# Gate operations of two groups moved from VectorE to GpSimd, and a new order for every step, in a recurrence followed by an MLP

## The chip, the cores and the metric

The kernel runs on one core of a Trainium2 chip. The core has TensorE (PE, which multiplies matrices; PEld is its loading of weights), VectorE (DVE), ScalarE (ACT) and GpSimd (POOL). SyncE (SP) issues all transfers here. Each engine runs its own queue in order, and engines wait for each other through semaphores. The metric is the time of one execution in device microseconds (us); lower is better.

## The reference

The first part is a recurrence with complex gates, on 4 batches, 8 heads, 768 tokens and a head size of 48. Its output is the input of the second part, an MLP of 3072 tokens, 384 to 2048 to 384, with a leaky rectifier.

```python
mag = np.sqrt(a_re * a_re + a_im * a_im)
scale = np.minimum(mag, 0.999) / (mag + 1e-06)
a_re_n, a_im_n = (a_re * scale, a_im * scale)
for t in range(S):
    new_re = ar * S_re - ai * S_im
    new_im = ar * S_im + ai * S_re
    kv = np.einsum('bhd,bhe->bhde', k[:, :, t], v[:, :, t])
    S_re, S_im = (new_re + kv, new_im)
    y[:, :, t] = np.einsum('bhd,bhde->bhe', q[:, :, t], S_re)
...
h = x @ w_in
g = np.maximum(h, 0.0) + alpha * np.minimum(h, 0.0)
return (g @ w_out).astype(np.float32)
```

The two weight matrices come as 64-bit floats and are made into 32-bit ones in the kernel.

## The kernel before, in words

A gate is split into a magnitude and a phase. The phases are multiplied up along the tokens, and keys and queries are turned by the products; what is left is a recurrence with real decays.

**Gates.** Nine groups of chunks of 128 tokens go through `gates`: in batch 0 one chunk (group 0), two chunks (group 1) and three chunks (group 2), and in each later batch two groups of three. A group loads its gates (L250), normalizes them on ACT and DVE (L253 to L301), multiplies decays into ever longer products (L318) and sends them out (L323, `decs`). Then it multiplies phases up in two levels. Seven pairs of a product (L338) and a sum (L340) run over eight neighbouring tokens; seven pairs of the same lines run over eight such blocks; a loop over the rest carries a running product from one block to the next (again L338 and L340, on `run`), with a copy of the carry from group to group (L381, L387). Then the offsets are multiplied in (L396, L399), scaled to length one (L407 to L411), and put on all tokens with large DVE products (L426, L429), which go out as `phs` (L431). Between these stand short ACT copies (L366, L368, L391, L405, L413). A helper, `small`, sends an operation of at most 80 elements per partition to the engine `tiny`, and a few tiny operations use `tiny_engine` at once; larger ones go to DVE.

**Units.** Each of the 24 chunks is a unit. It loads queries and keys (KQ, L579 and L581), phases (PP, L587, one buffer) and decays (T, L594, two buffers), and turns keys and queries (L661, L663). Then come six levels of block lengths 1 to 32: a DVE product with decays (L717), copies on ACT (L740, L756), products of keys and queries on PE (L678), and masks (L699 on ACT, L702 on DVE). Last come the transposed keys (L785, copied at L787 and L788), the update of the state (L797, L826, L829) and the output (L808 to L841), copied by ACT (L855) and sent to memory (L860, `ysc`).

**MLP.** Finished units are loaded again as `xT` (L873), in groups of one or two. For each group 16 blocks of features are made (L889, three matmuls each), rectified by ACT and DVE (L896, L898), and multiplied with the second weights (L908).

**Weights.** Sixteen pieces are loaded (L491), taken apart on ACT (L507 to L511) and POOL (L515) and put together on DVE (L517, L519).

**Order.** Each of these is a Python generator that yields before every step. A long string of letters, `ORDER`, names whose next step is recorded: A to I are the nine gate groups, J the loads of units, K half rows of the values, L the values, M the pieces of weights, N and O the two weights, P to m (that is P to Z, then a to m) the 24 units, n the loads of `xT`, o the MLP. The order of the string is the order of every engine's queue and of SP's queue. Nothing is reordered at run time: an instruction that waits holds up all behind it on its engine.

Of the kernel before, what the change touches and what calls it, by code (L numbers as in the profile page):

```python
# [27 lines left out]


ORDER = (  # L30
    "AAAAAAAAAAAAAAAAAAAAABAAAAJMJJMABBBMMBANJMMAOAAAAAAAAAAAAAAAAAALLLNBLAAAAAAAAAAALNAAAAAAAKKKKKKKLLLA"
# [4 lines left out]
    "CQRMLLNDCJQCNRNRLLCQCCLLLRMCQCQDQRJJOCOCKQODCCCCRDNQQQQCCQQQQQQJODMQLNNDQODDODoQEKoooooooDOoRooNDJoo"
    "oooooDRRQQRQLLoooDNoooLoRLLLLLDRLOQNQooQoQLooRRoRoDDoQDQDOOLDoooDDoRDELDLRRRRORRRRRJDooDDDDDDDRoooRN"
    "NooDDRooooooEoRDRRRRRDNDoDoESDSDRDJOSREKOoooooLnoLLKoRSoooRRRRSSOLLKLSSSooESRLooooooLRoSOLLoLJELLSoo"
    "NJSSSSoEoEESSDooDDooDDDDDDooooDDDDDDDKJREEoooDDDDooEDDDSDDoEooEoooSSSRSSSoLSooooJJSETSJSJJooKJSoEooo"
    "DDDDDDooDESDSoooSSSDDDSSJEEoEETSSSSDESSSoSSSTEoooooooJJoKoEooDSDTooooEoSoTUKTLoTTTLoooooooooLTLoLoDK"  # L40
    "UooooooLDDTDJJooooJJnKDDDoEEooooDooTTETooDooooooLUoooooooooEoTToooUUDDLoooooooDTooToooooooDLDUUUoooo"
    "ooUTUUooooooUoTTTTEoUUTTTTEooTTUToLLLLoooEEEToLooTTTTTTJJTTUoUUoTTUJoEooTETTTTTKEUUUUUFooooEUoooLLVo"
    "oEoUooLLLELULLUVUoTUTVooUEEoooEULLLLLoooUUUJJJFEEUUUUUJJVVVUVVooooVVVJoUUUUUVVooFVooooUooVVoVFFVVoFV"
    "LLVooEEEEEEEEEEEEEEEEoooEEEEoooooFFJoWVLLVWJFVoooJooooVooVVVVVWVoLVFooWoFoEEEoEVoVLWWLLLLLLELLVWVnVo"
    "oJJEEEEEEJJFWooFEEEEEoWWoFFVFVJVFWVVoFoVooooooEWEWFVLVLVWWVWVVVVoooLKLooLLLoLLLJFFWWoXoWLJoEEoEEELEo"
    "ooooEooJooWWoEWEWWWEoooWEoEoooWWooFoWoWFoooooEXWWoooooLXoFoooooFFXoLXXWWWWXXWXFEXWXWWWXJJoooooJXXJXF"
    "WXXFFFFoWWWWWoXoXooLoooWooooooXWLXXXXXooFoooXXFYoLLFFFFFFFoXXooXoXXoooLLLLLLLoooLLLYXXXJJXFJXFFFFFFF"
    "FFFFooXYGooXXXGooYoooXXnFYJXXYYoFooYYXXXXYGooooYJJJoooooooooooJJYFFFFooJoooJooYYYYLGGoGZYYoooooooGGo"
    "FFFFFFFooooFoYZoooFooFFoZooooZYYZYYZGYYZZoYYYoGZoYFFoYoooKKLLoYLLLLZLoLLLJLFFFFFLFLFFoZGGYoooooGZooG"
    "GoGGYYoYYJJYoKKYGooYFFoFKKYoYLYLYLFLLLLYYLLLLFGaGZoYZFYYYFZZLZGKooooZooooLLoZKooFFFFFoooooZZZZaZZZZZ"  # L50
    "ooooZZoooooZooZoooJJFFGnooJoZZZZZFFFLooLFFZLZoZJLLLoGoaaGooooooooaZZaaGGJoGoooaooaLHaHaooGGoooGGGooa"
    "ooooooooZZaZGGZZZoZaaaaaGGoooaHJoGoooooooaaaoaGGaaGaaaoooooGGaoLoaLoJoooooHHGboGGGGGGGaoHoaooLLobooL"
    "LoooooJHHabJabHaaaaaabaJbJJaJaJaHaaabbbbbbbbHKoooooooHoooooooJGGGGoGGbbbHbGGooocGGGGbJHoooooooooooJG"
    "GGKoooHbbccoooooooooobbccbGGGHcGbobbbGcGoooGGGGGGGGGHccooobbHGbGKLooooHHboobLLJLLLLLoLLLLLbLKnoobbcc"
    "cHbbHJbcbcGHHHbHHbbcJoHHLLLLLLooLoLJLLHHHcooooocccHHoooooooooHGGGGbbbbbbbboGccccccGGocGGooocLoooooGo"
    "cLoccooooocLLGoGHGGooocJoooocGcccccccccccccJcccooKdooHooHoooJJJoHHHoJooHHHodHHHHoooooooooooHHHHdHHHH"
    "HooHHdoodddJdJddddJJooeooooooooooooddoodddoooeoooddHHoooooooooHddeeeeoHHHHHLHHHHHHHLLLdddLLLLLdLLLLo"
    "JLooeeddddodooHHddoJJeoooHdddHdddddneoooHHoIddeeeeeoodeJfLfIHdHHdHeddddooooeHooooLLLLooooooJJoooIIoo"
    "oeooooIoooHoHHHooeeIoeeeHHHLfILoooHIooLooeIofHeJJoeooeooooIfffefoooeeLofoLoLoeLLLeeeeeeeeoJHfKHJJooo"
    "oooofeoILLfooIeeHffffKLLLfoeLooeeeeeooooooofoooooooofoooLoofKffgooooffffffIffLILLLLJooIgHooooLfLfooo"  # L60
    "IooIKKIIIIoffffIfJnJfJHgfgJofIJJooooooofoooooogIfggfgoLoooffIIfLfffIogoKoggooooooooooooohhoogooooggg"
    "ggoIhJhggoooooLoJoooooooooohhLJJooooghggggggghohogIILIIoogIoooggIogLLLLooooooIohhhhhooooLLLLgIoKKggg"
    "ggggggJJJhhooohogggLIoooooooooIIIIIIKKoooogoghoIoooooioooLooooiJJIIoooooonIIIoohhhoiioooIIIIIoIhhhII"
    "hhhLLLLLLLhhhiJiooILLLLLooIhJooohiohhooIIooooiiJhhhhhhIhIIiohooooiooLoLiLLLILiJIhhIhhhhhJiiIiiiiooII"
    "IIIIIIIoooooooooooLiiiiIoIooooohhiiiiiiooojiooIIIIoooooIIoLjJJjjLooooLIooLiLoLLIjjjooooIooijjjjIIooo"
    "ooooiiiIiIIiiooiLooioooLLLiLLILoLLLIIjoiiijjoiiiioooIiojoooooooooojjjoooooooonojjjoooojjLjjjjjoooooI"
    "jLjLLooooooojjoojjjjjjoooJJJJJoooJJoojJJjoooookokkJJoooooooooooojkjkLLjjjkjjojjkkoJkkoJJJkoookooooLL"
    "LooooooooJlJlkkooooooooookokklooklokooooooloolkkkkokkklllLooookookLkoloLJkoooooooooLLkLLkLoLoooollkk"
    "kkkkkkkkkkkkkoooooooooollllllooJoooooookkolooooollollmmnJJloooooooomooollooooooooollmllooooommlloooo"
    "ooooooLLoLLoLoooLLLLLoLLLLooooomooooooommmmmoooollllllooolloooooolllllllllmmoooooooooLooLLLoooommooo"  # L70
# [930 lines left out]
```

## Time and profile before

| | us |
|---|---|
| median of 3 runs | 854.49 (851.1 to 855.48) |
| the profiled execution, in all | 854.34 |
| its span | 852.6 |
| PE busy | 697.3 (82%) |
| DVE busy | 653.5 (77%) |
| ACT busy | 439.1 (52%) |
| POOL busy | 209.2 (25%) |
| DMA packets | 57.1% of 16 queues' span, 129.20 MB |

The profile is of one execution. It tells the busy time of each engine, in the whole and in 40 equal slices of the span (one digit a slice, in tenths), the clock that was granted to PE, groups of instructions with their line, engine, tiles and shape, their number, total time and mean time, the idle time before them and what ended it, and the chain of work that ended last. An idle engine that is not the bottleneck costs nothing.

### The profile page before, as it was taken

To read this page: it belongs to the slowest core of one execution; us is meant where nothing else is said; L and a number is where in the kernel's file an instruction comes from. 1 tells how busy PE (TensorE), PEld (TensorE's weight loads), DVE (VectorE), ACT (ScalarE), POOL (GpSimd) and SP (SyncE) were. 2 spreads that over 40 slices of the span, in tenths; PEclk is the share of its full clock that TensorE was granted. 3 is DMA by queue.
4 is the path that set the end of the run, shared out by engine and by line. 5 is a ranking of instruction groups with operands and counts; after the bars stand their busy time and mean duration, and the time that the engine had idled before them with its cause. 6 is when DMAs were issued, how large, how long until landed. Compare 5 with 4: busy or idle time off the path is not lost.

```text
span 852.6 us, 26860 instructions
## 1 busy us (share of the span) xinstructions
PE 697.3 (82%) x11488; PEld 529.4 (62%) x11488; DVE 653.5 (77%) x1020; ACT 439.1 (52%) x937; POOL 209.2 (25%) x293
## 2 busy tenths in 40 slices
PE   0001314776998899889999999999999999999998
PEld 0001313565776677667777777777777777777776
DVE  5999999997996899599989997887776846633212
ACT  6767758766355754474576436554344334322221
POOL 6131232376403710260056144000052000000000
PEclk9999656798998999999999999999999999999999
DMA  8687876755768365756765766667454555412010
GB/s 238 155 272 188 263 200 189 216 128 138 203 174 199 102 182 163 209 133 156 231 156 145 212 162 177 157 182 185 113 130 104 148 143 117 102 46 65 11 39 9
DMA packets 194174, 130.91 MB, mean 154 GB/s; under 512 B 74120, under 2 KB 185864, under 8 KB 194056
## 3 DMA queue, kind: packets, MB, share of 16 engines
q1 hardware_dynamic: 194056, 129.20, 57.1%
q8 instruction: 90, 1.47, 0.7%
q14 instruction: 28, 0.23, 0.1%
...
## 4 chain that ended last, share of the span: by engine, by line
PE 63%; DVE 18%; POOL 6%; ACT 5%; DMA 4%; issue 3%; SPq 0%; DVEq 0%; ACTq 0%; POOLq 0%
PE ps_o L908 26%; PE ps_h L889 24%; PE ps_lv L678 4%; POOL gate L338 3%; PE ps_y L817 3%; DVE KQ L717 3%; PE ps_kv L797 2%; PE ps_y L841 2%; DVE gate L338 2%; DVE gate L426 2%; DMA T<-decs 2%; POOL run L340 2%; DVE gate L340 1%; PE ps_kt L785 1%; POOL gate L340 1%
## 5 line engine op out<-in xcount | busy, mean ns | idle before, releaser
L908 PE MATMUL ps_o<-w_out_sb,g_sb 128*128 128x384 f32 x768 | 297.9, 500 | 11.7 <-DVE g_sb L898 9.0
L889 PE MATMUL ps_h<-xT,w_in_sb 128*128 128x256 f32 (+1 forms) x1344 | 301.2, 357 | 0.0
L889 PEld LDWEIGHTS ps_h<-xT,w_in_sb 128*128 128x128 f32 x1344 | 235.1, 193 | 72.2 <-issue 3.3
L898 DVE SCALAR_TENSOR_TENSOR g_sb<-g_sb,al,ps_h 128x256 f32<-128x256 f32 (+1 forms) x224 | 97.3, 436 | 133.4 <-ACT g_sb L896 132.7
L896 ACT ACTIVATE g_sb<-ps_h 128x256 f32<-128x256 f32 (+1 forms) x224 | 79.1, 354 | 203.7 <-PE ps_h L889 202.7
L908 PEld LDWEIGHTS ps_o<-w_out_sb,g_sb 128*128 128x128 f32 x768 | 137.9, 192 | 63.0 <-DVE g_sb L898 12.0
L717 DVE TENSOR_TENSOR KQ<-KQ,T 96x1024 f32<-96x1024 f32 x120 | 146.6, 1225 | 33.9 <-PE ps_lv L678 22.9
L678 PE MATMUL ps_lv<-WQ 96*32 96x32 f32 x2304 | 34.3, 202 | 80.4 <-DVE WQ L661 51.8
L678 PEld LDWEIGHTS ps_lv<-WQ 96*32 96x32 f32 x2304 | 26.5, 115 | 98.1 <-DVE WQ L661 51.8
L338 POOL TENSOR_TENSOR gate<-gate 128x72 f32<-128x72 f32 x42 | 26.3, 626 | 148.3 <-ACT gate L368 145.5
L740 ACT COPY WQ<-KQ 96x1024 f32<-96x1024 f32 x48 | 50.0, 1041 | 15.4 <-DVE KQ L717 15.1
L515 POOL TENSOR_SCALAR top<-top 128x768 f32<-128x768 f32 x16 | 39.3, 2461 | 70.0 <-ACT top L507 59.7
L338 DVE TENSOR_TENSOR gate<-gate 128x576 f32<-128x576 f32 (+5 forms) x84 | 50.5, 601 | 1.7
L756 ACT COPY W<-KQ 96x512 f32<-96x512 f32 x48 | 30.8, 642 | 40.6 <-DVE KQ L717 33.1
L855 ACT COPY T<-ps_y 48x256 f32<-48x256 f32 x96 | 30.7, 366 | 36.8 <-PE ps_y L841 36.2
L817 PE MATMUL ps_y<-A,VL 64*48 64x64 f32 x2304 | 42.3, 227 | 3.7 <-issue 3.7
L785 PE MATMUL ps_kt<-ident,KQ 96*128 96x96 f32 x192 | 26.4, 264 | 22.2 <-DVE KQ L717 12.2
L426 DVE TENSOR_TENSOR gate<-gate 128x1152 f32<-128x1152 f32 (+2 forms) x36 | 44.2, 1250 | 0.1
L699 ACT ACTIVATE A<-ps_lv,columns 128x64 f32<-128x64 f32 x144 | 37.4, 337 | 13.0 <-PE ps_lv L678 12.9
L817 PEld LDWEIGHTS ps_y<-A,VL 64*48 64x48 f32 x2304 | 40.6, 128 | 4.4 <-issue 4.4
L785 PEld LDWEIGHTS ps_kt<-ident,KQ 96*128 96x128 f32 x192 | 22.1, 150 | 31.1 <-ACT T L788 10.9
L678 PE MATMUL ps_lv<-KQ,W 96*32 96x32 f32 x1536 | 24.2, 204 | 17.9 <-ACT W L756 17.9
...
## 6 DMA issues: line engine op xcount, KB each, us to landing
...
```

The lines of the kernel that those rows point to most:

```text
L338: on(4 * k).tensor_tensor(out=m, in0=w[:, 1::-1].unsqueeze(2).to_broadcast([P, 2, 2, k]), in1=pairs_of(u), op=ALU.mult)
L426: TT(out=m[:, a], in0=U5[:, 1 + a], in1=turned(off3, o)[:, a].unsqueeze(1).unsqueeze(3).to_broadcast([P, L // 2, nb, 2]), op=ALU.mult)
L515: nc.gpsimd.tensor_scalar(out=top, in0=top, scalar1=F64_SMALL, scalar2=None, op0=ALU.max)
L678: nc.tensor.matmul(t[64 * i + j:64 * i + j + HC // 2, p], lhsT=keys(n, g), rhs=queries(n, g), start=True, stop=True)
L717: nc.vector.tensor_tensor(out=x, in0=x if x0 is None else x0, in1=m, op=ALU.mult)
L740: nc.scalar.copy(z.rearrange("p i n t -> p i (n t)").rearrange("p i (m h) -> p m i h", h=h), bass.AP(tensor=KQ.tensor, offset=KQ.offset + ...
L785: nc.tensor.transpose(t[:, p], KQ[:, 1, 4 * i + p], ident[:D2, :D2])
L817: nc.tensor.matmul(o, lhsT=Vp[h][64 * i:64 * i + 64, s, e_ * D:(e_ + 1) * D], rhs=a, start=False, stop=False)
L889: nc.tensor.matmul(p, lhsT=w_in_sb[:, f // 2, kk, f % 2 * P:(f % 2 + 1) * P], rhs=x_of[m][:, kk], start=(kk == 0), stop=(kk == NK - 1))
L896: nc.scalar.activation(gt, p, AF.Relu, scale=-1.0)
L898: nc.vector.scalar_tensor_tensor(out=gt, in0=gt, scalar=al_1[:, f:f + 1], in1=p, op0=ALU.mult, op1=ALU.add)
L908: nc.tensor.matmul(sums[0], lhsT=gt[:, c * P:(c + 1) * P], rhs=w_out_sb[:, f], start=(f == 0), stop=(f == NF - 1))
```

## The change

The test that picks the engine for tiny operations asks for the first group instead of the first batch. So groups 1 and 2, which are the rest of batch 0, do their operations of at most 80 elements on POOL, as all groups of the later batches already do; group 0 stays on DVE. And the whole of `ORDER` is another string: every queue has a new order. No tile, buffer, shape or transfer is changed.

```diff
 ORDER = (
-    "AAAAAAAAAAAAAAAAAAAAABAAAAJMJJMABBBMMBANJMMAOAAAAAAAAAAAAAAAAAALLLNBLAAAAAAAAAAALNAAAAAAAKKKKKKKLLLA"
-    "OALLAMNNAAAAAAOAAAAAAAAABLBNAAAAAAALAANBBNOOBNBBBLBMBBBJOJNOBBBBBNBBJNNNBBNBBBBOBBBBBBBBBBBBBBBNOPBP"
...
+    "AAAAAAAAAAAAAAAAAAAAAAAAAAMMMAAMMJBBBBAMBJNNNNAAAAAAAAAAAAABABNANAAAAAABAAAABBABBNNAABBMBBABBNAAAABB"
+    "BBBKBAAKKBJNABAKBAKAKAKAKOKNKJKKKKAAAAKOBBBANAABKABOMAABMAAAAABABAAABAAOOOOOOOBNNOOBBNOONNBNMNNNBJJB"
...
-        tiny, tiny_engine = (DVE, nc.vector) if b == 0 else (POOL, nc.gpsimd)
+        tiny, tiny_engine = (DVE, nc.vector) if g < 1 else (POOL, nc.gpsimd)

         def small(k, *after):
             return tiny(k, *after) if k <= SMALL else DVE(k, *after)
```

Here `g` is the number of the group and `b` that of the batch.

More of the change, by code (lines that the diff above doesn't have):

```diff
@@ L30 @@
 ORDER = (
-    "AAAAAAAAAAAAAAAAAAAAABAAAAJMJJMABBBMMBANJMMAOAAAAAAAAAAAAAAAAAALLLNBLAAAAAAAAAAALNAAAAAAAKKKKKKKLLLA"
-    "OALLAMNNAAAAAAOAAAAAAAAABLBNAAAAAAALAANBBNOOBNBBBLBMBBBJOJNOBBBBBNBBJNNNBBNBBBBOBBBBBBBBBBBBBBBNOPBP"
-    "OBPPPPCCCBOKBBBBBBBBBBBBBPPOBBPKBCBBBMPCBPKKBCBJKKOPOPBBBBBBOMBKPNPMBBKNJBCKBBBBPPMBKKNKKBBNBPBBBBPP"
-    "BCCBPPOPCCCPPPNNPPCCCCPPCPPPPJLPPPPPJNCJPCNNNCCNCNCCQJQJPQJDDJJCPCJMNCNCPCPCPPCOCQQPDQDDJPPPPOCOOOCK"
-    "QCQCCCCCCQQCCCCCMOQCOJCJRCCRCOQOCOQQCQCOOOCCCCCCNNKKMMCCOCQCRCQCQCNNNKCLLLLLLQLCCCCCRQOCnCDCCCOCOCCC"
@@ L36 @@
[L36 to L70, printed above, removed]
@@ L71 @@
-    "oooooooooooooLoooooomoooooomooooLLLLLLLLmooonooooooooooommommooooooooooooooooooooooooommmmmmoooooooo"
-    "ooooooooommmooooooooooooooommmmmmmmmmmmomoommnoooooooooooooooooooooooooooooooooooooooooooooooooooooo"
+    "AAAAAAAAAAAAAAAAAAAAAAAAAAMMMAAMMJBBBBAMBJNNNNAAAAAAAAAAAAABABNANAAAAAABAAAABBABBNNAABBMBBABBNAAAABB"
+    "BBBKBAAKKBJNABAKBAKAKAKAKOKNKJKKKKAAAAKOBBBANAABKABOMAABMAAAAABABAAABAAOOOOOOOBNNOOBBNOONNBNMNNNBJJB"
+    "BBBBOPJPONPPPPPNMNPPOOPOOOPPCCLLMMMLLLLBLLJBCBBBPBBBBBBBJJBBBBBBBBBBBBBPPPPPPNOBCCCPCPPPBBNKCKKKKKCK"
@@ new lines @@
+    "LLKLBBBBBOBLLPPPPPPPPBBBBBBBPCCCCCLCBBNCCJBBBBPPPOBOOOOCPPPPBCMJDDCCNCCOCOCPCJCNCOOCJJJCOCONNNNCCCPD"
+    "DKCQCCCCCDDNCLLLLCQDCCQCCCCCCCCCCCOQLNLPPPPPPMQMQQQQPPPPJQQLODDQQQODJJOJJJJJJQQQDDQCQCCDCCQDCQRKCOKL"
+    "CLLLLLLKnRRRQRQRQQQQQQQQQQRQRQQRCCCCCQCQCRCNNNDDCDDoDQooDoooLLLoooQoDMoLQooCDDDCoRCoCoCDoooooNRoNNCo"
+    "CoKNCCCCLLLRRRoooooLLLLLLDRLRRQQCCCCCCCRKKRMKCCRRoQCDooCQQQQRRoRRQCCoooooCoCoDDDRRRRRRRRRRoDoRJORoDR"
+    "oDOOOOODRJJEJNDoooooLLDRRRRoRRRRDoSoOooSDSooDLoooJoLLooSSDSEoooSJooDooonoSSoDoSSDNNNSLLENoDoSSSoooLN"
@@ new lines @@
+    "DLooooSDooRSSSEJoJooOOoooooSSSoJLESoTESSSSLoLLLoTSJoooJSSSJooJSoJJooooSSSSSSooDESSEKTKESSESSSSSSDSoo"
+    "UDUooTTTDoDTDoDDDDDDKooDDDDoooooooTDTTTLEoEToooELLTTTTTooooLoooJoJoTTooooEoUTTTTTTTTooooooUUTToUTTLT"
+    "EELLLLLLLLDDDDDDEEEDDDDDDDDLoooDDDDDDoTooTTTTooTLnLLLEEoooEUULLLLLLLKoTooooooEoLUEoooLoToDDUoTDooDUo"
+    "DDDDooooooooUEoEEUUoEEEDTToTTTTTooToUoUoUoooUooDUooooDooooUUUUUUUUUoooooDDDUoDooUoUUooooEUUUUUUoDoEo"
+    "oEoEoooJUJUUUUUEUEJEEJJoooooEJEoEJooooEoEooEUooEooEoooooVoooooooJEoVooVoVoooooVFFJJJooooUVJVVVFoEEoE"
@@ new lines @@
+    "EooEoEEEEEEVEVEnooJJVVELEEEoooooooLVoWWVVooLoLoLLFFVoooVVoooVWoLoEoooLoEooVLoWEWWVWoVEoVVVVoEoWLWLWE"
+    "WLooEoFLVVVEVLoooVJJoVEoooVEJEJJWEEEEEoEFVVVVVVoWWVVVWFFFooELELoEooWFFFFFoooooLoWWLLLLLLWLoEoooooLEo"
+    "EEEEoEoELLLoWWVVVVVVVEWVWWooooEoEooooJJEJooWoXWWWEFJWWEooooooWWoooooWWWWWWWWXWLLLWWWWWWWXFFooWoLLooL"
+    "LXXXXoXooooXXXoJJJooooGXooooLXoFFFoGXXXXooooLXXooFoFooFoXYXoFXGonooooJJooLLGoYXXXooooXXXoXXoFLoLLFFF"
+    "FYFooFoXYFoXoGYYYFYXYooFFooJJooFYoYooooooFKoJooJXXXXYXXLXXXXXGXXXXooFoXFooooFGoGooFFFFFFFFFFJJFJYYYY"
@@ new lines @@
+    "FooooYooYYooZoZZZoFooLoFLLLLooLLFLLFGLooooLooYYYYYLYLYoZYZZZZoooooKKKYKYooYooYooJooFFYFGKFFGZGJJGYYY"
+    "YYYYYYYYLooLLoLFGKGoYYYYYYoZoKZoKooooooJoFLoFLFGoFGFFFoFFoFFFFFFFFFFoLLLZZZZnLZZZLooLLKooooLFFooooZo"
+    "FZZooFFZFZFFoFoFJJFoJooFoFFooZZZJZJZoFZooooZZooZZZZZZZZZZZZFLLLFoaZZZZZaoooooooooooJaJJooaoGoooaaaaa"
+    "ooooaoooooaoooGaaaaaaaaoooobooooGJGooLGoGGJGGaaaaaaaJJaLLLaGoGoooGoLLLLbbbbHHooooooaoooLoabLooaGGooG"
+    "aaaaaaGaGaGHbbbHbGbHKbKGJaJaaooooooGGboooooooaoaaaGGaGoJoobbbboooGbbGbGGGGoGGGbcoooooooooLooLobLLLbL"
@@ new lines @@
+    "LLHJLbLJLcbLbboobooocoHobooooHHHooocobbbooocccccobbooLcnooLooooJJJHbbHHHbobbbbooLoHLLLHGccLLoLLLLLGL"
+    "LHoGoooHoGooJGooHGboooooGoocGccGcGbGGGGbbGcGcGcGoooobobbobGJoooGGGGooGGGccccGGGGcoocccooLdccocoooodc"
+    "ococccccccccccbbooJJLLGGGGGGGJJJGJcodcHcLLGococcHGGGoGoGooooooooLLoLoLoodooooodHGGdHoGodddddKKooHLLL"
+    "LoKooHoooodoooddddJodLHLHoHddooJooHooHooddHooonodddHdoodddddooooHHHHHHHooooddIIoooodHHoddddJdddJddLH"
+    "JdHdedddHHddeJJJoJJJJJJHooooooooooeooHoooooeeeeeeHeoeooooofooeooooofeeoeffeooeoooLLoooooJeoeooooooLe"
@@ new lines @@
+    "oeeeeeeffooogHHHHHHfHHHHHHHHHHHHHfHHHHHHHgHeeeeLLLLLLLLLLIKoooooeooeefeeeeeeeKeeeeeKeeeeHHooHooooofo"
+    "ooJoHHHHfHJLLoLfoLHHLLLLoooLLooLffJJffIoILofLoLfofooooogoooogfgffffgfggfoffooooogggIoffooooooHHHHHHo"
+    "HoooofIKooHHooofffffKKfngfHHofggggIIooKKLooooLLLLLLggLLLLgoLHoooggggggggoffffoffffooHofggfgoooooooHo"
+    "ooooJJogooooLoooooIIgoooIJIIIIJoJgJJgggggggggohooIggggoIIoooooooIohhoogLLLLJJhhJJJoohoooooohhoooIooh"
+    "hooohohoooohooonohoioIohhhhhohooiihoooooooooooJohiihiooIihIhhhIIIIhLoohooooKhoooohhLLoLLLLLILLIoIIIh"
@@ new lines @@
+    "oooiiihihhhhhhhhhhhhhhhhLoLhioooIooooooLLLLLooioiiioooiioioooIoooooiJiiiJooJJJLJJIIIIIIooooojoIoIooo"
+    "ooIooIooojjIIIoIIIIoLIIoIIoIiijiiiiioooooooLojjLoLLoioLooioiIIIIiIIIIIIiIIIIIiiILLjLLLLLLLLojjjoioiI"
+    "iioooojojooooojjioiIooIIiIIIIoILoojjjjojoooiILjjojiiioLLIIIIIIIIoIioooonjjjjjjjjooooIooIIooIooIooIoo"
+    "oojooooojjjjjjjjjjjjjjjJJJJJjooooooojoooooJJJJoooookkLkoooooookoJooooookkoookkoookkoLojokokoookkkkko"
+    "oJkoJJJJJkoooooookookkkkkkLLllLLoLLLLLoookkooLkLoooLkokookkkkkkkkkkkkkkklkokoooooooookLooooLllLllLLo"
@@ L73 @@
+    "nooooooololllJJloooooooJJooooooooLLoLollooomlollooolloooooooommmooooooomomolllolooooooommmmmoooLoLLL"
+    "llllLooloooLmooommlmmoolloooooolollllllllllLlmllollloooooooooooooooooooomoooomoooooooooooooooooLLLLL"
+    "LLooooooolooommmmmmoooooooooooomoooooooooooooomnoooooLLLLLooommmooooooomoommmmmmmmmmmmoooooooooomooo"
+    "ommmoooooooooooonooooooooooooooooooooooooooooooooooooooooooooooooooooooooooooooooooooooooooooooooooo"
     "oooooooooooooooooooooooooooooooooooooooooooooooooooooooooooooooooooooooooooooooooooooooooooo")
```

## The prediction

> **What bounds the kernel now.** I read the page first, then the busy time by stage, the groups by form, the order of time on POOL, and the chain. All times are on the span's clock.
>
> ```profile
> span 852.6 us, 26860 instructions
> PE 697.3 (82%) x11488; PEld 529.4 (62%) x11488; DVE 653.5 (77%) x1020; ACT 439.1 (52%) x937; POOL 209.2 (25%) x293
> PE   0001314776998899889999999999999999999998
> DVE  5999999997996899599989997887776846633212
> POOL 6131232376403710260056144000052000000000
> ```
>
> DVE is full in the first 190 us, PE from about 215 us on. The stages, with the columns time, then busy us and instructions of PE, PEld, DVE, ACT, POOL, then the granted clock, say it in us:
>
> ```profile
> 110.00:147.00 37.00, 10.70 (x335) 9.38 (x324) 36.38 (x64) 27.35 (x43) 10.44 (x4) 0.53 0.63 187
> 215.00:260.00 45.00, 44.57 (x842) 34.57 (x844) 44.35 (x70) 20.23 (x56) 9.08 (x6) 1.00 0.75 199
> 260.00:300.00 40.00, 33.95 (x687) 25.44 (x678) 30.34 (x40) 25.91 (x53) 25.73 (x34) 0.89 0.57 141
> 400.00:500.00 100.00, 99.97 (x1703) 75.58 (x1702) 93.66 (x133) 55.06 (x119) 32.41 (x49) 1.00 0.71 191
> ```
>
> From 400 to 800 us PE has no hole. So the end is PE's 697.3 us of work plus its 155 idle us: 123 up to 147 us, where the MLP has just begun (first L889 at 144.7), 18 up to 215, 11 from 215 to 400, 3 after 800. Only idle PE time, and time at a low clock (0.89 and 0.95 between 260 and 350, some 7 us), can be won.
>
> What a moved operation costs, by form:
>
> ```profile
> L338 POOL TENSOR_TENSOR gate<-gate 128x72 f32<-128x72 f32 x42 | 26.3, 626 | 148.3 <-ACT gate L368 145.5
> L340 POOL TENSOR_TENSOR run<-gate 128x6 f32<-128x6 f32 x36 | 25.5, 707 | 2.8
> L338 DVE TENSOR_TENSOR gate<-gate 128x72 f32<-128x72 f32 x7 | 2.2, 315 | 0.1
> L340 DVE TENSOR_TENSOR run<-gate 128x6 f32<-128x6 f32 x12 | 2.6, 216 | 0.2
> ```
>
> POOL's means hide two prices. In order of time on POOL (batch 1) the same form takes 0.23 us, and 5.53 us where DVE is full of two-input instructions; on DVE, two equal instructions, the second beside POOL's L515:
>
> ```profile
> 191.79 0.23 POOL L338 TENSOR_TENSOR gate<-run,runs 128x12 f32<-128x12 f32 x1 [0.44 <-ACT runs L368]
> 195.87 5.53 POOL L338 TENSOR_TENSOR gate<-run,runs 128x12 f32<-128x12 f32 x1
> 17.59 0.36 DVE L338 TENSOR_TENSOR gate<-gate 128x192 f32<-128x192 f32 x1
> 18.27 0.87 DVE L338 TENSOR_TENSOR gate<-gate 128x192 f32<-128x192 f32 x1
> ```
>
> **The change, part by part.**
>
> (1) 71 small instructions leave DVE (34 of group 1, 37 of group 2). By form 17.9 us go: 20 in the two run loops at 0.20 and 0.22, 28 products and sums at 0.18 to 0.32, 23 others at 0.16 to 1.07. POOL gets them: by its mean rows 51.6 us (forms of group 1 at the nearest row of group size 3). At each form's shortest they would be about 22 us, at the rate of the slowest chains (14 operations in 15.9 us from 175.4, 12 in 15.5 from 276.2) about 85. I take the mean rows for group 1, whose DVE neighbours become sparse, and 1.1 us each for group 2, whose DVE is full. Does POOL slow DVE? In the whole trace 21 DVE instructions are over 0.25 us above their form's shortest, 10.5 us in all, 15 of them beside an L515. No L515 is added, so I add 1 us for two more L409, between 0 and 5.
>
> The Trainium skill's page "SBUF — State Buffer" (section "The single rule") says that a GpSimd operation and a DVE one with two SBUF inputs take turns at a shared port pair, the second blocking fully. Our rows show the blocking, mostly with POOL as the loser. If DVE lost the 22 us instead, the move would cost DVE 4 us net, and the estimate by the page would be some 4 us slower than no change.
>
> (2) The new order, early. I add up by form what stands ahead on DVE in each built order. Ahead of unit 0's first multiplication (L661, 50.5 us) are now 44.4 us of work, not 42.0, with five weight limbs (L519) for three, and its phases leave later: 54 us. Between unit 0's first and last L717 there are now 13.9 us of DVE work for 28.8. That stretch took 26.9 us; in later units, with DVE free, 16.0 (unit 8), 16.7 (14) and 18.4 (11). I take 17.5, so it ends near 75 for 80.4.
>
> Group 1's chain starts on POOL near 55: 14 operations 8.3 us, the carry's copy 1.0, a run loop of 8 at 0.74 5.9, one L515 2.5, then 3.4 and 3.0, and ACT's copies between, about 2: DVE's L426 for group 1 comes at 81 instead of 68.8. Behind this wait stand, on ACT, unit 0's copies of the transposed keys (L787: second half 88 for 84.9); on SP, group 1's phases and all behind them. Unit 1 then begins at 102 for 87.9, its first L717 at 111 for 91.2. But between unit 1's first and last L717 DVE now has 18.6 us of work for 41.5, so the last comes near 130, as before (129.8).
>
> SP: unit 0's output (L860) left at 96.8; now ACT's copies of it (L855) wait behind copies for group 2 that need DVE, so about 114. From it to the load of xT SP has 22 issues, before 18, which took 25.8 us: 127 at 0.6 us an issue, 145 at the old rate. The MLP begins between 140 and 148, before at 144.7. Group 2's POOL chain is priced high, and a zeroing for group 3 (L305), which waits for DVE, stands inside its run loop in POOL's order; its L426 comes at 157 for 132.6, but unit 3 needs it only at 172.7: 176. Unit 3's output, before at 211, falls near 214, with nearly the same MLP work behind it (54 and 16 matmuls of L889 and L908 for 57 and 17, 1.3 us). **Sum of the start: +3 us, between -6 and +15.**
>
> (3) From there PE carries. The 11 idle us from 215 to 400 and 7 of low clock are 18. DVE has less queued at each unit (197.5 to 173.8 us of work ahead of unit 4, 295.2 to 285.1 of unit 8, 349.4 to 335.0 of unit 10), so waits on DVE should shrink. Waits for transfers are in the chain too, and DVE cannot shorten them:
>
> ```profile
> 255.32 7.41 DMA T<-decs
> 356.31 5.62 DMA KQ<-in_q_dram
> ```
>
> I take half of the 18: **-9, between 0 and -18.** After 400 there is nothing to win. Tighter places are new: the keys' product (L797) stands within 1.5 us of PE work behind the last transposition in 18 of 24 units, before in 7. What lies between is two copies, 483 and 279 ns: 0.8 us. So 0, up to +9 (18 times 0.5 us). Nothing else is added: PE's, ACT's and SP's instructions are the same in number, the transfers the same 129.2 MB.
>
> Sum: 3 - 9 + 0 = -6. The profiled execution has 852.6 us of span and took 854.3 in all, 0.2 under the median of 854.5; so about **848 us**.
>
> **Rivals.**
> - *No change that shows (854).* Start +3 and a gain of 3. For it: the waits in the chain after 215 are for DMA and "issue" as much as for DVE. Against it: DVE is at 44.4 of 45 us where the idle time follows.
> - *POOL's chain becomes the start's bound (863).* Place: group 1's POOL chain, where DVE's two-input instructions hold it off. At the slow rate its 14 take 15.9 for 8.3 us and its 8 take 10 for 6: +12 on unit 1, little of it absorbed, as the MLP then starts past 155. +3, +12, less a gain of 6: +9. It decides once L426 of group 1 begins later than about 90 us. Against it: unit 0's L717 leave DVE half empty just there.
> - *The tighter order stalls PE in the steady part (860).* +3 at the start, +9 from L797, -6 gained. For it: ACT's queue is in order and busy 55 of 100 us at 400. Against it: before's seven close places made no hole after 400.
>
> **How the numbers follow.** A measurement of this kernel tells 0.5%, 4.3 us, from no change. Forecast 0.46 (its own range 838 to 850), no change 0.22, POOL's chain 0.20, the tight order 0.12. Faster 0.46, same 0.22, slower 0.32. The range runs from 834 (start -3, the 18 us nearly all won) to 864, the worst rival; about 0.1 lies beyond each end.
>
> **What would show it.** Right: L426 of group 1 near 81 and the first L889 at 140 to 148; DVE visibly idle within 57 to 75; PE's idle time from 215 to 400 near half of 11 us with the clock near 1.0. Wrong: POOL operations of group 1 over 1 us each, the first L889 past 155, unit 3's output past 220, or holes in PE after 400.

## The result, and the profile after

The changed kernel takes 843.56 us, the median of 11 runs (842.05 to 850.05); the kernel before, run beside it on the same chip, 851.15 us (11 runs, 847.05 to 855.48). The ratio is 0.9915, with a 95% interval of 0.989 to 0.9939. So it is faster, by 0.85%. The forecast was 848 us, 4.4 us too high, inside its own range of 838 to 850. Of these 4.4 us, 3.3 come from the base: the forecast started from 854.49 us, the median of 3 runs, and the median of 11 is 851.15. The sum was nearly right; two of its three terms were not.

The profiled execution took 845.45 us. These are the lines of its page that answer to those shown of before: the span, busy time and number of instructions of each engine, and the span in 40 slices.

```profile
span 843.7 us, 26844 instructions
PE 698.8 (83%) x11488; PEld 529.6 (63%) x11488; DVE 645.2 (76%) x949; ACT 440.5 (52%) x937; POOL 244.8 (29%) x364
PE   0002317778899999998999999999999999999998
DVE  5987998989898998887998898795878756642212
POOL 5375668628216400340124312500003400000000
```

PE is busy for about as long as before (698.8 for 697.3 us); its idle time (span less busy time) has gone from 155.3 to 144.9 us. DVE has 71 instructions less and POOL 71 more. In the PE row the seventh slice (127 to 148 us) has 7 tenths for 4, and the slices from 256 to 298 us have 9 for 8. The stages, in the order time, then busy us and instructions of PE, PEld, DVE, ACT, POOL, then the granted clock:

```profile
110.00:147.00 37.00, 18.89 (x500) 15.33 (x500) 33.92 (x43) 27.52 (x47) 31.83 (x33) 1.00 0.73 188
215.00:260.00 45.00, 42.23 (x677) 33.34 (x678) 42.81 (x64) 22.33 (x58) 10.34 (x15) 1.00 0.64 176
260.00:300.00 40.00, 39.66 (x708) 30.37 (x708) 37.06 (x49) 27.51 (x55) 20.63 (x31) 1.00 0.58 140
400.00:500.00 100.00, 99.73 (x1638) 73.50 (x1637) 88.88 (x123) 57.41 (x123) 27.79 (x44) 1.00 0.64 166
500.00:600.00 100.00, 95.64 (x1689) 72.26 (x1687) 78.26 (x104) 48.13 (x114) 17.79 (x38) 1.00 0.68 171
```

From 110 to 147 us PE does 18.9 us of work where it did 10.7: this is the gain of the start, which I had not forecast. (The 1.00 in that row is not a clock that was recorded; the last section tells why.) From 260 to 300 us it is busy 39.7 us for 34.0, at a clock of 1.00 for 0.89: the forecast gain. From 500 to 600 us it is busy 95.6 for 100.0: something is given back.

**A measure of the lead.** Idle time alone does not tell the lead, because at a low clock PE is busy for longer with the same work. So I gave each matmul a price, the spacing of equal matmuls that follow each other in the trace at full clock (L889 0.432 us, its narrow form 0.22, L908 0.645, the small ones of the units 0.035 to 0.13), and summed the prices of the matmuls begun by a certain time. The table shows how much more work PE has done than in the profiled execution of before, in us. The prices add up to 738 us for the whole kernel, 6% above PE's busy time, so the entries depend on them, the early ones most, where the small matmuls are many. With the mean spacings from 400 to 800 us as prices (644 us in all) the row of after reads 5.3, 6.0, 18.1, 16.6, 14.2, 9.1 and 8.2. The lead at 800 us agrees with the difference of the spans to within 2 us in eleven of the thirteen rows; in the two blends (e9, e10) it misses 2.4 and 5.0 us of the loss.

| execution | 147 | 215 | 350 | 400 | 500 | 600 | 800 us | span before less span |
|---|---|---|---|---|---|---|---|---|
| after | 6.3 | 9.4 | 19.8 | 17.3 | 17.0 | 10.8 | 10.4 | 8.9 |
| e1: move, old order | -5.0 | -5.8 | -2.5 | -8.5 | -9.3 | -10.0 | -9.3 | -9.0 |
| e11: group 1 moved, old order | -1.8 | 2.4 | 4.1 | 4.3 | 3.7 | 3.4 | 2.0 | 1.2 |
| e2: new order, no move | 0.6 | 1.9 | 13.7 | 14.8 | 11.7 | 5.2 | 6.1 | 4.5 |
| e7: new order, group 1 moved | 3.5 | 5.3 | 17.6 | 16.7 | 17.4 | 11.5 | 11.1 | 9.3 |
| e8: new order, group 2 moved | 3.2 | 5.3 | 17.6 | 16.3 | 16.5 | 10.8 | 10.4 | 8.8 |
| e3: joint at 350 us | 7.1 | 9.4 | 21.3 | 11.1 | 10.4 | 9.8 | 9.9 | 9.4 |
| e4: joint at 190 us | 7.1 | -3.6 | -1.7 | -1.7 | -2.9 | -3.8 | -3.3 | -3.5 |
| e5: joint at 390 us | 7.1 | 9.4 | 20.9 | 14.1 | 11.9 | 12.2 | 11.9 | 11.2 |
| e6: joint at 430 us | 6.9 | 9.4 | 20.5 | 17.3 | 3.9 | 4.2 | 3.1 | 2.4 |
| e9: short blend | 7.1 | 9.4 | 20.5 | 17.9 | -4.1 | -5.3 | -3.6 | -6.0 |
| e10: long blend | 7.1 | 9.4 | 18.2 | 16.3 | 1.0 | -12.2 | -10.6 | -15.6 |
| e12: before again | 0.0 | 0.2 | 0.0 | 0.0 | -1.5 | -2.2 | -1.5 | -1.6 |

The row of after gives the account that the prediction has to stand against: +9.4 us by 215 us, +7.9 from there to 400 us, -6.9 from 400 to 800 us (with the lower prices +6.0, +10.6 and -8.4).

**Where the start's gain lies.** In both kernels the first matmul of the MLP stands in PE's queue behind unit 1's work. In order of time on PE, the kernel before (start, duration, instruction, and in brackets the idle time ahead and what ended it):

```profile
129.84 0.90 PE L785 MATMUL ps_kt<-ident,KQ 96*128 96x96 f32 x4 [5.43 <-DVE KQ L717]
138.25 0.90 PE L785 MATMUL ps_kt<-ident,KQ 96*128 96x96 f32 x4 [7.52 <-ACT T L788]
...
144.65 1.67 PE L889 MATMUL ps_h<-xT,w_in_sb 128*128 128x128 f32 x12
```

The same view of the kernel after:

```profile
129.62 0.90 PE L785 MATMUL ps_kt<-ident,KQ 96*128 96x96 f32 x4
131.25 0.90 PE L785 MATMUL ps_kt<-ident,KQ 96*128 96x96 f32 x4 [0.74 <-ACT T L788]
...
137.56 1.79 PE L889 MATMUL ps_h<-xT,w_in_sb 128*128 128x128 f32 x12
```

Unit 1 reaches its transposition at the same time, 129.8 and 129.6 us. Before, the second half then waited 7.5 us for the copy of the first (L787, L788); now it waits 0.7. The steps from there to the first L889 take 6.4 and 6.3 us, and the MLP starts 7.1 us earlier. The change has not done away with such waits: unit 0's transposition, behind which no MLP work stands yet, now waits 6.1 us for its copy at 81.2 us, and before 2.6. The copy of unit 1 was late because of what stood ahead of it in ACT's queue. The kernel before, in order of time on ACT:

```profile
132.81 1.16 ACT L264 ACTIVATE gate<-gate 128x1152 f32<-128x1152 f32 x1
...
134.31 1.17 ACT L267 ACTIVATE gate<-gate 128x1152 f32<-128x1152 f32 x1
135.36 1.04 ACT L740 COPY WQ<-KQ 96x1024 f32<-96x1024 f32 x1
136.30 1.17 ACT L511 ACTIVATE w_in_sb<-g_sb,columns 128x768 bf16<-128x768 f32 x1
...
137.56 0.48 ACT L787 COPY T<-ps_kt 128x384 f32<-128x384 f32 x1
```

Gate work, a weight piece and another unit's copy run first; in the new order L787 follows at 130.56 us. Unit 3 has the same fault in another form: a gate's short copy on ACT waits for POOL, and the unit's copy stands behind it (before, ACT):

```profile
204.74 0.22 ACT L366 COPY runs<-run 128x36 f32<-128x36 f32 x1 [5.63 <-POOL gate L338]
...
205.12 0.47 ACT L787 COPY T<-ps_kt 128x384 f32<-128x384 f32 x1
```

After, unit 3's two L787 run at 193.06 and 194.35 us without such a wait, and its last matmul of L841 begins at 199.2 for 211.0 us. What the copy in the kernel before waits for is the last product of POOL's run loop, which ends at 204.7 us; the operation of 5.53 us that the prediction showed stands earlier in that loop (195.87 to 201.40) and takes up 2.3 us of the wait. Over the whole execution, ACT's waits for POOL were these in the kernel before (total us, times, longest):

```profile
ACT runs L366 <- POOL gate L338: 12.0, 3, 5.6
ACT runs L366 <- POOL gate L340: 3.3, 1, 3.3
```

and these in the kernel after:

```profile
ACT gate L413 <- POOL gate L411: 8.8, 5, 2.8
ACT gate L405 <- POOL gate L399: 2.7, 1, 2.7
ACT runs L366 <- POOL gate L340: 1.9, 2, 1.6
```

The 15.3 us at L366 have become 1.9, though POOL has 71 more operations in these chains; with the waits at L413 and L405, which are new, the sum is 13.4. So the sum alone does not tell the gain; what stands behind each wait differs.

**What is given back.** PE's waits from 400 to 800 us in the kernel after; before had none there:

```profile
PE ps_lv L678 <- ACT W L756: 1.8, 1, 1.8
PE ps_h L889 <- issue: 1.5, 1, 1.5
PE ps_y L817 <- issue: 0.8, 2, 0.5
PE ps_y L817 <- DMA VL<-vsc: 0.5, 1, 0.5
```

These are 4.6 us, in five places that have nothing in common. L797, where I had put this risk, is not among them. The other 2.3 of the 6.9 us are not placed; e12, the kernel before itself, falls by 1.5 us in the same stretch.

### The profile page after: what moved, and what is told of

The parts are those of the page before. It is cut to its first block, busy times and chain, and to the rows that moved or that the text cites. A ratio compares the mean times of both kernels' runs of the same rounds, so it can differ in the third digit from the quotient of the medians.

```text
span 843.7 us, 26844 instructions
## 1 busy us (share of the span) xinstructions
PE 698.8 (83%) x11488; PEld 529.6 (63%) x11488; DVE 645.2 (76%) x949; ACT 440.5 (52%) x937; POOL 244.8 (29%) x364
## 4 chain that ended last, share of the span: by engine, by line
PE 72%; DMA 8%; DVE 7%; ACT 6%; issue 3%; POOL 2%; SPq 2%; DVEq 0%; ACTq 0%; POOLq 0%
PE ps_h L889 28%; PE ps_o L908 28%; PE ps_lv L678 5%; PE ps_y L817 4%; PE ps_kv L797 3%; PE ps_y L841 2%; DMA T<-decs 2%; DMA phs<-gate 2%; PE ps_kt L785 2%; DVE KQ L717 1%; DMA gate<-in_a_im_dram 1%; POOL gate L318 1%; DMA St<-in_v_dram 1%; DVE gate L338 1%; DVE gate L259 1%
## 5 line engine op out<-in xcount | busy, mean ns | idle before, releaser
L908 PE MATMUL ps_o<-w_out_sb,g_sb 128*128 128x384 f32 x768 | 295.7, 499 | 12.0 <-DVE g_sb L898 8.7
L889 PE MATMUL ps_h<-xT,w_in_sb 128*128 128x256 f32 (+1 forms) x1344 | 302.2, 357 | 3.1 <-issue 3.1
L889 PEld LDWEIGHTS ps_h<-xT,w_in_sb 128*128 128x128 f32 x1344 | 234.3, 194 | 76.3 <-issue 7.2
L908 PEld LDWEIGHTS ps_o<-w_out_sb,g_sb 128*128 128x128 f32 x768 | 138.0, 192 | 63.9 <-DVE g_sb L898 11.8
L717 DVE TENSOR_TENSOR KQ<-KQ,T 96x1024 f32<-96x1024 f32 x120 | 149.1, 1244 | 31.7 <-PE ps_lv L678 22.7
L338 POOL TENSOR_TENSOR gate<-gate 128x72 f32<-128x72 f32 (+1 forms) x56 | 41.0, 732 | 118.6 <-ACT gate L368 114.8
L338 DVE TENSOR_TENSOR gate<-gate 128x576 f32<-128x576 f32 (+3 forms) x70 | 45.5, 651 | 1.2
L318 POOL TENSOR_TENSOR gate<-gate 128x72 f32<-128x72 f32 (+5 forms) x24 | 21.9, 911 | 76.8 <-DVE gate L318 74.4
L426 DVE TENSOR_TENSOR gate<-gate 128x1152 f32<-128x1152 f32 (+2 forms) x36 | 42.8, 1219 | 1.3 <-POOL gate L411 1.2
L515 POOL TENSOR_SCALAR top<-top 128x768 f32<-128x768 f32 x16 | 37.1, 2321 | 22.3 <-ACT top L507 22.3
L702 DVE TENSOR_TENSOR A<-ps_lv,mask 128x256 f32<-128x256 f32 x96 | 36.8, 412 | 0.0
```

The lines of the kernel that those rows point to most:

```text
L338: on(4 * k).tensor_tensor(out=m, in0=w[:, 1::-1].unsqueeze(2).to_broadcast([P, 2, 2, k]), in1=pairs_of(u), op=ALU.mult)
L426: TT(out=m[:, a], in0=U5[:, 1 + a], in1=turned(off3, o)[:, a].unsqueeze(1).unsqueeze(3).to_broadcast([P, L // 2, nb, 2]), op=ALU.mult)
L515: nc.gpsimd.tensor_scalar(out=top, in0=top, scalar1=F64_SMALL, scalar2=None, op0=ALU.max)
L702: nc.vector.tensor_tensor(out=a.rearrange("p n (g t) -> p n g t", g=2), in0=t.unsqueeze(2).to_broadcast(whole), in1=masks[name].rearrange( ...
L717: nc.vector.tensor_tensor(out=x, in0=x if x0 is None else x0, in1=m, op=ALU.mult)
L889: nc.tensor.matmul(p, lhsT=w_in_sb[:, f // 2, kk, f % 2 * P:(f % 2 + 1) * P], rhs=x_of[m][:, kk], start=(kk == 0), stop=(kk == NK - 1))
```

## The experiments

Each was timed in five rounds against the kernel before on the same chip, unless said otherwise; the median of before was 849.78 us beside e1 to e4, 850.81 beside e5 to e8 and 851.58 beside e9 to e11.

### The two parts apart: e1 and e2

e1 has the move without the new order:

```diff
 # ORDER as before
-        tiny, tiny_engine = (DVE, nc.vector) if b == 0 else (POOL, nc.gpsimd)
+        tiny, tiny_engine = (DVE, nc.vector) if g < 1 else (POOL, nc.gpsimd)
```

> The order string of before, with the small gate operations of groups 1 and 2 on POOL. Theory 1 (the gain of after belongs to the order; the old order has DVE's consumer of group 1, L426, close behind operations that were quick on DVE and are slower on POOL): POOL's 14 operations of group 1 fall among full DVE work and take 12 to 16 us, L426 of group 1 comes at 75 to 85 us instead of 68.8, DVE waits there, the first L889 is late by 3 to 10 us, and the time is 852 to 862 us against 851. Rival (DVE bounds the start, so 17.9 us less on DVE help in any order): first L889 at 135 to 140 us and 842 to 846 us.

Measured: 861.31 us, ratio 1.0139 (1.0098 to 1.018). The move alone costs 12 us. What DVE waits for from 85 to 147 us in this kernel:

```profile
DVE top L517 <- POOL top L515: 7.6, 2, 4.2
DVE gate L426 <- POOL gate L411: 5.0, 1, 5.0
```

and from 50 to 85 us, the two longest:

```profile
DVE gate L259 <- ACT gate L257: 5.3, 1, 5.3
DVE gate L426 <- POOL gate L411: 2.1, 1, 2.1
```

The size was as theory 1 had it and the place only in part. The wait of L426 of group 1 is short (it begins at 71.8 us, not 75 to 85). The longest is one that I had not named: the weights' L515 on POOL, which have nothing to do with the gates, stand in POOL's queue behind and within group 2's chain, and DVE's L517 and all behind it wait for them. The 5.3 us at L259 are of the same kind: ACT's L366 for group 1 waits for POOL, and the other group's L255 and L257 stand behind it on ACT. The first L889 comes at 152.8 us for 144.6, and the path to it shows a further wait, on ACT. The halves of unit 1's transposition are 14.0 us apart here, 8.4 in the kernel before and 1.6 in the kernel after. The copy in between stands on ACT behind a copy of group 2, which waits for POOL (PE, then ACT, of e1):

```profile
147.09 0.90 PE L785 MATMUL ps_kt<-ident,KQ 96*128 96x96 f32 x4 [13.10 <-ACT T L788]
134.60 0.22 ACT L366 COPY runs<-run 128x36 f32<-128x36 f32 x1 [6.66 <-POOL gate L338]
```

e2 is the opposite, the order without the move:

```diff
 # ORDER as after
-        tiny, tiny_engine = (DVE, nc.vector) if g < 1 else (POOL, nc.gpsimd)
+        tiny, tiny_engine = (DVE, nc.vector) if b == 0 else (POOL, nc.gpsimd)
```

> The order string of after, with the small gate operations of groups 1 and 2 left on DVE as in before. Theory 1 (the order holds the gain): DVE has free time between 50 and 85 us in this order and takes the 34 operations of group 1 there; the first L889 stays at 135 to 142 us, and the time is 840 to 848 us. Rival (the move pays): the 17.9 us on DVE come back on the path of the start; the first L889 at 143 to 152 us and 849 to 856 us.

Measured: 848.75 us, ratio 0.9997 (0.9971 to 1.0023); the first L889 at 143.3 us. Theory 1 fell: the order alone is worth nothing that can be measured, and the move in it is worth about 0.8% (0.9915 for 0.9997). The rows of e2 and of after in the table differ by 5.7 us at 147 us and by 2.5 to 7.5 at later times, 4.3 at 800 us: the move is worth some 5 us, and it is won before the MLP starts. The order alone already takes the wait of 7.5 us away (PE of e2):

```profile
135.38 0.90 PE L785 MATMUL ps_kt<-ident,KQ 96*128 96x96 f32 x4
137.02 0.90 PE L785 MATMUL ps_kt<-ident,KQ 96*128 96x96 f32 x4 [0.74 <-ACT T L788]
```

But it brings unit 1 there 5.5 us later than the kernel before (135.4 for 129.8 us), and the move brings it back (129.6). So the earlier start of the MLP needs both parts. In e2 L661 of unit 1 begins at 105.1 us, in after at 99.6, and L661 of the units 2 to 7 is later by 5 to 7 us, too. The order's own row is +0.6 at 147, +14.8 at 400 and +5.2 at 600 us.

So the parts do not add: the move alone is +1.4%, the order alone 0, both together -0.85%.

### Group by group: e7, e8 and e11

e7 moves group 1 alone in the new order, e8 group 2 alone, e11 group 1 alone in the old order.

```diff
-        tiny, tiny_engine = (DVE, nc.vector) if g < 1 else (POOL, nc.gpsimd)
+        tiny, tiny_engine = (DVE, nc.vector) if g in (0, 2) else (POOL, nc.gpsimd)   # e7, and e11 with before's ORDER
+        tiny, tiny_engine = (DVE, nc.vector) if g < 2 else (POOL, nc.gpsimd)         # e8
```

> After's order, with only group 1's small operations on POOL (group 2's on DVE as in before). With both on DVE, unit 1's first multiplication (L661) began at 105.1 us, with both on POOL at 99.6, and that lead of 5.5 us was kept to the end. Theory (group 1's move gives all, since the lead is there before group 2's chain starts): L661 of unit 1 at 99 to 101 us, first L889 at 137 to 139.5 us, 843 to 846 us. Rival (both halves take some 9 us from DVE and each gives half): first L889 at 140 to 142 us, 846 to 848 us.

> After's order, with only group 2's small operations on POOL. Theory (group 1's move gives all): L661 of unit 1 at 104 to 106 us, first L889 at 141 to 144 us, 847 to 850 us. Rival (each half gives half): first L889 at 140 to 141 us, 845 to 847 us.

Measured: e7 845.65 us, ratio 0.9946 (0.9918 to 0.9974), first L889 at 139.6 us, L661 of unit 1 at 100.7. e8 847.24 us, ratio 0.9964 (0.994 to 0.9988), first L889 at 140.7, L661 of unit 1 at 103.9. The times do not tell theory and rival apart: both lie within theory's ranges, and that of e8 is at the edge of them. The first L889 speaks for the rival, that each half gives its share: against e2 it is 3.7 us earlier in e7 and 2.7 in e8, of 5.8 in after, where theory wanted all from group 1. (The start comes out alike from one execution to the next: in e12 below it is within 0.2 us of before.) In the medians, against e2, group 1 gives 0.51%, group 2 0.33%, and both 0.82%, which is nearly their sum, but the intervals overlap; and by 800 us the rows of e7, e8 and after stand at 11.1, 10.4 and 10.4 us. So that the two shares add up is shown for the start alone. A reading that fits: DVE is nearly full from 85 to 147 us in e2 (24.5 of 25 and 35.0 of 37 us), so work taken from it counts wherever it was.

> Before's order with only group 1's small operations on POOL (group 2's on DVE). With both on POOL in this order, DVE waited from 85 to 147 us 7.6 us for the weights' L515, which stand behind the gate chain in POOL's queue, and 5.0 us for group 2's L411. Theory (group 2's chain is what costs in the old order, by holding up L515): L517 waits under 2 us, the first L889 comes at 144 to 148 us, and the time is 848 to 854 us. Rival (already group 1's chain, which makes DVE wait 7.4 us before 85 us for 9 us of work taken away, sets the loss): first L889 at 149 to 153 us, 856 to 862 us.

Measured: 853.71 us, ratio 1.004 (1.0012 to 1.0069), the first L889 at 147.9 us, and no wait of DVE for POOL from 85 to 147 us: the 7.6 us of L517 and the 5.0 us of L426 are gone. The halves of unit 1's transposition are 8.4 us apart, as in the kernel before. Theory held: some two thirds of the 12 us that the move costs in the old order (861.31 less 853.71 us) are group 2's chain, which shares POOL's queue with L515 and holds up ACT's copies. The 5.3 us of L259 are still there; group 1 on POOL costs 0.4% here, and gives 0.5% in the new order.

### Keeping the lead: e3, e4, e5, e6, e9 and e10

After is ahead by 17 to 20 us at 350 to 400 us, and gives back some 6 between 500 and 600 us, where before's order has no hole. Four kernels take after's order up to a letter and go on in before's:

```diff
+def joined(p, r):            # letters p, then those of r that p has not used
+    need, out = Counter(p), []
+    for c in r:
+        if need[c] > 0: need[c] -= 1
+        else: out.append(c)
+    return p + "".join(out)
-ORDER = AFTER
+ORDER = joined(AFTER[:1812], BEFORE)                    # e3, up to unit 10
+ORDER = joined(AFTER[:AFTER.index("T")], BEFORE)        # e4, up to unit 4
+ORDER = joined(AFTER[:2052], BEFORE)                    # e5
+ORDER = joined(AFTER[:2259], BEFORE)                    # e6
```

> After's order up to the first letter of unit 10 (some 350 us), then the remaining letters in before's order; the move as in after. PE has done 19.8 us more of its work by 350 us in after than in before, and loses 9 of them again from 350 to 600 us. Theory (the loss belongs to after's order of that stretch, for which before's has no hole in PE): the lead is kept, PE is idle for under 2 us from 400 to 800 us, and the time is 833 to 839 us. Rival (the lead itself brings PE to places where transfers and copies are not yet ready, whatever the order): PE idle 4 to 8 us from 400 to 800 us, and the time is 841 to 847 us.

> After's order up to the first letter of unit 4 (some 190 us), then the remaining letters in before's order; the move as in after. PE was ahead by 2 us at 190, 9 at 215 and 15 to 20 at 300 to 350 us in after. Theory (the gain from 215 to 400 us belongs to the order of that stretch): PE's idle time from 215 to 400 us is 9 to 13 us as in before, and the time is 845 to 850 us. Rival (it is the relief of DVE in the start that is cashed in later): PE's idle time from 215 to 400 us is 5 to 8 us as in after, and the time is 836 to 843 us.

> After's order up to a later joint in unit 10 (letter 2052, some 390 us), then the remaining letters in before's order; the move as in after. In the earlier joint at the first letter of unit 10, 17 steps of a gate group that before's order had long recorded fell together at the joint, and PE lost 12.7 us of its lead between 350 and 375 us; from 400 to 800 us it lost nothing more. Here 5 steps of a gate group are overdue and 19 of the MLP ahead. Theory (after's order of 400 to 600 us gives back 6 us, and this can be avoided): PE's idle time from 400 to 800 us is under 2 us, the joint costs 0 to 4 us, and the time is 835 to 841 us. Rival (what is given back is the lead itself, met by a limit in any order): 842 to 847 us with PE idle for over 4 us from 400 to 800 us, or again a loss at the joint.

> The same with the joint at letter 2259 (some 440 us), where 15 gate steps are overdue and 11 steps of the MLP are ahead. Theory: the loss after 500 us is avoided, the joint costs 0 to 6 us, 836 to 843 us. Rival: as in after, 842 to 847 us.

Measured: e3 846.73 us, ratio 0.997 (0.9944 to 0.9996); e4 857.69, 1.0099 (1.0067 to 1.013); e5 845.56, 0.9941 (0.992 to 0.9962); e6 851.54, 1.0007 (0.9984 to 1.0029). None beats after.

One half of the theory held. Behind the joint before's order loses next to nothing: from 500 to 800 us 0.5 us in e3, 0 in e5, 0.8 in e6, where after loses 6.6 and e2 5.6. So the loss after 500 us belongs to the new order's later part, and the lead itself does not bring it about. The other half fell: the joints cost 7 to 13 us, as much as was to be saved or more. (The rival of e5 had allowed for this, and its 842 to 847 us came.) They cost it in three different ways. In e3 a gate's copy on ACT waits for POOL and holds up a unit's copy (ACT of e3):

```profile
359.06 0.22 ACT L366 COPY runs<-gate 128x36 f32<-128x36 f32 x1 [7.66 <-POOL gate L340]
...
359.31 0.63 ACT L756 COPY W<-KQ 96x512 f32<-96x512 f32 x1
```

and PE waits for that copy (PE of e3):

```profile
359.98 0.66 PE L678 MATMUL ps_lv<-KQ,W 96*32 96x32 f32 x32 [5.70 <-ACT W L756]
```

In e6 the overdue gate steps fill DVE's queue, with 3.7 us among them in which DVE itself waits for a gate step on ACT (L267), and PE waits for one MLP step behind them (PE's waits of e6 from 425 to 450 us):

```profile
PE ps_h L889 <- DVE g_sb L898: 9.1, 1, 9.1
```

In e4 they fill ACT's: PE waits 9.5 us for one copy of the MLP (L918), ahead of which nine instructions of a gate group run on ACT from 193.2 us on; e3's way is there too, a wait of 4.9 us for POOL at L366. The expectation of e4 had a question of its own, whether the gain from 215 to 400 us belongs to the order there. PE's idle time from 215 to 400 us is 10.0 us, in the range of the theory; but the time is above both ranges, as the joint at 190 us lost 13 us, and so the run decides little. e2, which has that gain without the move, decides it for the order.

e9 and e10 spread the change from the one order to the other:

```diff
+for c in AFTER's letters, k-th occurrence of c at x in AFTER and at y in BEFORE:
+    w = min(1, max(0, (x - lo) / (hi - lo)))            # e9: lo, hi = 2000, 2500; e10: 2050, 3050
+    key = max(key of occurrence k - 1, x + w * (y - x))
-ORDER = AFTER
+ORDER = letters sorted by key
```

> After's order up to letter 2000 (some 385 us), before's order from letter 2500 (some 530 us), and between them each step at a place that goes gradually from its place in the one to its place in the other; the move as in after. At the hard joints PE lost 6 to 13 us, because the gate steps that before's order has by then recorded fell together in DVE's queue and the units' and the MLP's steps stood behind them. Theory (spread out, these steps fit into DVE's free time, 11 us from 400 to 500 us and 22 from 500 to 600): PE's idle time from 385 to 800 us is under 3 us, and the time is 835 to 841 us. Rival (before's order of the gates can't be joined to after's lead at all, the lead over before is the gate work put off): PE loses 5 to 10 us between 385 and 530 us, 843 to 848 us.

> The same with the passage from letter 2050 (some 390 us) to letter 3050 (some 650 us). Theory (spread out, the gate steps cost nothing): PE's idle time from 390 to 800 us is under 3 us, 835 to 841 us. Rival (the 6 us that after gives back from 500 to 600 us are the put-off gate work itself, which is still late here): PE idle 4 to 7 us from 500 to 650 us, 842 to 846 us.

Measured: e9 859.46 us, ratio 1.0101 (1.0059 to 1.0143); e10 868.45, 1.0213 (1.0184 to 1.0243). Both theories fell, and the rivals were too mild. PE's waits of e9 from 385 to 500 us begin with these:

```profile
PE ps_lv L678 <- ACT W L756: 4.6, 2, 2.7
PE ps_y L817 <- DMA VL<-vsc: 3.7, 1, 3.7
PE ps_lv L678 <- DVE KQ L717: 1.7, 1, 1.7
PE ps_y L841 <- DVE St L829: 1.6, 1, 1.6
```

From 400 to 500 us PE is busy 86 of 100 us, DVE 80, ACT 50 and POOL 29. No engine is full; the queues wait for each other. The rule moves each step by its own amount, so steps that were neighbours in both orders can be torn apart. That an order is good for what stands beside what, and not for how early each step is on the whole, would explain both runs; it is not shown, and which pairs matter was not tried.

### How firm the profile of before is: e12

e12 is the kernel before, unchanged, profiled once more.

> The kernel of before, unchanged, profiled a second time. The prediction counted 11 idle us of PE from 215 to 400 us and 7 us of low clock there from one execution, which took 854.3 us at a mean clock of 0.951; the 24 executions of before with a mean clock of at most 0.955 have a median of 852.9 us, the 51 others one of some 849. Theory (part of the 18 us belongs to that execution and not to the order: after a hole PE's clock is down for a while): an execution at a clock above 0.956 and 845 to 851 us loses 3 to 8 us less than 18 from 215 to 400 us, and the start, up to 215 us, is the same within 2 us. Rival (the holes belong to the order): 16 to 19 us lost from 215 to 400 us, and what is faster lies in the start.

Measured: 855.94 us at a mean clock of 0.954, so the run was not of the kind that the theory speaks of, and it decides nothing between them. It shows something else: the two executions are alike, in PE's work within 1 us at every time of the table up to 400 us, and with the same stages from 215 to 400. In e12:

```profile
260.00:300.00 40.00, 33.27 (x728) 25.13 (x722) 30.68 (x41) 26.49 (x54) 25.80 (x34) 0.94 0.63 149
300.00:350.00 50.00, 47.68 (x791) 35.60 (x789) 44.85 (x65) 20.74 (x50) 7.33 (x20) 0.95 0.68 185
```

Both executions are 4 to 5 us above the median of before of some 850 us. In which stage the others are faster stays open. The slower ones go with a lower clock: of 75 executions timed beside these experiments and listed with their clock, the 24 with a mean clock of at most 0.955 have a median of 852.9 us and the 30 from 0.956 to 0.97 849.65. Which of the two brings about the other is not shown. The 21 above 0.97 (848.88) can't be ranked with them; the last section tells why.

## Why the prediction was right in its sum and wrong in its parts

The sum was +3 for the start, -9 from 215 to 400 us, 0 after 400. The profile has -9.4, -7.9 and +6.9 us by the table (with the lower prices -6.0, -10.6 and +8.4).

**(1) The move.** The step held in its direction; what was mis-sized is what POOL does to DVE. DVE was to lose 17.9 us by its rows, and the 71 operations took 17.1 in e2. But between e2 and after its busy time differs by only 10.6 us (655.8 to 645.2), and the path by 5.5. POOL was to gain 51.6 us and gained 66.2 between e2 and after (178.6 to 244.8), but only 36 between before and e1 (209.2 to 245.1), because the same operations of POOL cost so much less in the new order: the groups of the run loop, in e2,

```profile
L340 POOL TENSOR_TENSOR run<-gate 128x6 f32<-128x6 f32 x36 | 16.2, 449 | 2.8
L338 POOL TENSOR_TENSOR gate<-run,runs 128x12 f32<-128x12 f32 x36 | 15.4, 429 | 33.0 <-ACT runs L368 30.6
```

have the same 36 operations at 449 and 429 ns that took 707 and 772 ns before. The bounds for POOL, 22 and 85 us, held all of this. DVE's loss to POOL was put at 1 us, between 0 and 5. In the same order it is 3.4 to 3.7: instructions of DVE over 0.25 us above the shortest of their form are 14 with 7.2 us in e2 and 21 with 10.6 in after (before had 21 with 10.5), and all that were not moved took 3.7 us longer in after. The rest of the difference in busy time is not accounted for. The estimate that the prediction made from the Trainium skill's page "SBUF — State Buffer" (section "The single rule"), with DVE as the one that loses the 22 us, is not what these rows show.

**(2) The start.** Most of its times were right. Forecast and measured: unit 0's stretch of L717 ends near 75 (74.1), L426 of group 1 at 81 (80.2), unit 1's L661 at 102 (99.6), its first L717 at 111 (110.2), its last ends at 130 (129.4), L860 of unit 0 at 114 (112.7), the load of xT between 127 and 145 (131.6). L426 of group 2 came at 151.4 for 157, unit 3's L661 at 171.6 for 176. The step that failed is the next: I let the MLP's start follow from the load of xT, 140 to 148 us for 144.7 before. In both kernels PE's queue has unit 1's transposition and output ahead of the first L889, and before, this stretch held a wait of 7.5 us for ACT's copy. I had unit 1's last L717 at an unchanged 130 us and did not follow the path from there to L889, which was 16 us before (from the start of that L717, 128.6 to 144.6) and is 9.4 now. Unit 3 is the same mistake: I gave it its old 38 us from L661 to output, and it took 27.6; ACT's wait for POOL is 5.6 of the 10.7 us that went. The sum of the start was bounded by -6, and the profile is at that bound or past it (-6.0 to -9.4).

The places where L797 and L788 follow the transposition closely, 18 of 24 units for 7, I had read as a danger. PE's waits for these copies are 17.2 us in all before and 15.5 after, so the danger did not come, and nor did a gain on the whole. The gain is in units 1 and 3, where the new order puts ACT's copies directly behind the transposition and the next stage stands behind them.

**(3) From 215 to 400 us.** -9 was forecast, half of 11 idle us and 7 us of low clock; -7.9 was measured, made up otherwise. From 260 to 350 us nearly all is won: idle time 8.5 to 1.6 us, and the clock is at 1.00 for 0.89 and 0.95; the lead grows from 5.0 us at 260 to 19.8 at 350 us. Before and behind, some is lost: idle 0.4 to 2.8 us from 215 to 260, 2.2 to 3.0 from 350 to 400. The reason given, less work queued on DVE at each unit, does not fit: e2 has the gain here (+12.9 between 215 and 400 us) with the 71 operations still on DVE. The gain belongs to the order; which of its steps bring it was not tried.

**After 400 us.** 0 was forecast with up to +9; 6.9 us were given back (8.4 with the lower prices). The size is inside the bound, the place is not L797.

**The rivals.** POOL's chain as the bound was to give 863 us. It did not happen in the change, where L426 of group 1 begins before 90 us. The time of e1, 861 us, is near the rival's, but not by the rival's way: L426 of group 1 begins at 71.8 us there, and what costs is group 2's chain, through L515 in POOL's queue and the copies on ACT, which the rival did not name. No change that shows is what the order alone gives (848.75 beside 849.78 us). Against the tight order, PE's holes after 400 us stand at other lines.

So the forecast of 848 us came within 5 us by luck: the start was 9 to 12 us better than its step, the part after 400 us 7 to 8 us worse, and the base 3.3 us too high. The change was forecast at -6 us; it is -8.9 between the two profiled executions and -7.6 between the medians.
